# The first head pair of a chunk-selecting attention kernel ordered by hand, with the preparation of the next two pairs among its steps

## The chip, the cores and the metric

The kernel runs on one core of a Trainium2 chip. The metric is the device time in microseconds (us) of one execution. Five engines run their own instruction queues in order: PE (matrix products and transposes), DVE (vector), ACT (scalar functions), POOL (GpSimd) and SP, which here only issues transfers. Weights are transferred by DMAs that POOL issues, queries, keys and values by DMAs that SP issues.

## The reference

Attention over 4 batches, 8 heads, 768 positions, head dimension 64, in which each query sees only its six best key chunks of 32; then a layer in which each token goes to one of eight experts.

```python
k_min, k_max = k_chunks.min(3), k_chunks.max(3)
ub = sum(maximum(q * k_min, q * k_max))          # per query and chunk
ub = where(causal, ub, -1e9)
top_chunks = argsort(ub)[..., -6:]
scores = 0.125 * q @ k.T
scores = where(chunk chosen and causal, scores, -1e9)
attn_out = softmax(scores) @ v
x = attn_out, heads side by side                 # 3072 x 512
e = argmax(x @ w_gate)                           # one expert per token
out = softmax weight * relu(x @ w1[e]) @ w2[e]
```

## The kernel before

**Tiling.** The 32 heads are handled as 16 pairs (NP = 16, four pairs to a batch), numbered by `i`. A pair's keys, queries and values come as 128 x 6 x 2 x 64 tiles, each by two loads of 192 KB (L199 to L203). There is one buffer for keys and one for queries, so the load for the next pair can begin only when PE has transposed the present one; values have two buffers.

**Steps of a pair.** They are the functions of `prep_steps` (L205 on). `k_t(hf)` transposes half of the keys on PE into a PSUM tile (three buffers, tag "m", shared by most steps). `k_red` takes the chunk maximum and minimum on DVE, `k_out` copies the keys into KTE on ACT. `q_t` transposes queries, `q_v` copies them (DVE), `q_r` takes their positive part (POOL), `q_c` and `q_s` write both heads into QSB (POOL, ACT). `kse` prepares the chunk bounds (DVE), `ub` multiplies with them (PE, eight passes, L320) and copies the result (ACT). `select_t`, `select` and `mask` choose six chunks: transposes (PE), `max` (DVE), transposes again, and two copies into the mask rows of QSB (ACT). `mask_rows` writes the matching rows of KTE once per buffer.

Then come seven units per pair: `scores(i, u)` (PE, exponential on ACT, causal masking on POOL for units 0, 1, 5 and 6), `av(i, u)` (product with the values, PE), `add(i, u)` (sum for the denominator, DVE), `out_t` (DVE), and the router steps of the pair before (`ud`, `lgp_t`, `lgp`, `x_t`, `xr`).

**Order.** In the main loop (L779 on) PE and POOL run in the order in which the code is written (`manual_schedule(engines={PE, POOL})`); the other engines' order is found by a scheduler. The loop does, for pair i, its own scores, the selection for pair i + 1 and the key and query preparation for pair i + 2. `keys(j)` is the key part of that, and issues the load of the keys of pair j + 1.

**The prologue** (L740 to L778) comes before the loop, with POOL, DVE and ACT in written order too. `consts_first` starts nine matrix products on zeros (`warm_up`), builds identity, iotas and causal offsets, and clears buffers. `first` transposes pair 0's keys and queries. `consts_pool` makes further constants on POOL, `ub` and `select_first` handle pair 0's selection in two halves, so that scores of the first half (`scored`) run between them. Then pair 1's keys and queries are prepared whole, and `consts_last` ends it. The loop's pass for i = 0 has its own branches: no work of an earlier pair, and `keys(2)` after `out_t`.

**Weights.** `load_w` (L180) moves a quarter of one expert's weights (512 KB as bf16, converted on the way) by a DMA from POOL; 32 of them fill `w_all`. `weights(slot)` (L707) issues those that fall in a slot; the 44 slots lie four to a pair, in pairs 0 to 13 except 5, 9 and 13. All 32 are spread evenly over them. After the last pair the expert stage gathers token rows and multiplies them with the weights.

Of the kernel before, what the change touches and what calls it, by code (L numbers as in the profile page):

```python
# [24 lines left out]
def kernel(  # L25
# [32 lines left out]
    W1W = WE // 2  # L58
    DC = 2 * E
    CW = 64  # L60

    const = ctx.enter_context(tc.tile_pool(name="const", bufs=1))
    dram = ctx.enter_context(tc.tile_pool(name="dram", bufs=1, space=bass.MemoryType.DRAM))
# [54 lines left out]
    def warm_up():  # L118
        wb = work.tile([128, 512], BF16, tag="Pr", bufs=4, name="wb")
        nc.vector.memset(wb[:], 0.0)  # L120
        pw = ps_o.tile([128, 512], FP32, tag="o", name="pw")
        for n in range(9):
            nc.tensor.matmul(pw[:], lhsT=wb[:, 0:128], rhs=wb[:], start=True, stop=True)

    def consts_first():
        warm_up()
        nc.gpsimd.memset(warm[:], 0.0)
        nc.scalar.activation(warm[:], warm[:], AF.Exp)
        masks.make_identity(nc, ident_f[:])
        iota(iota_p[:], [[0, 1]], mul=1)  # L130
        iota(colc[:], [[1, NCH], [0, CH]])
        iota(iota_c[:], [[1, NCH]])
        zero_half(KTE[0])
        nc.gpsimd.memset(KS[0][:], 0.0)
        nc.gpsimd.memset(KD[0][:], 0.0)
        zero_half(QSB[0])
        nc.gpsimd.memset(nsel[:].rearrange("p t h a n -> p (t h a n)").bitcast(FP32), 0.0)
        nc.vector.tensor_scalar(pm64[:], iota_p[:], 64.0, None, ALU.subtract)
        nc.vector.tensor_scalar(chunk_p[:], iota_p[:], 32.0, None, ALU.is_ge)
        nc.vector.tensor_scalar(tmp_p[:], iota_p[:], 64.0, None, ALU.is_ge)  # L140
        nc.vector.tensor_tensor(chunk_p[:], chunk_p[:], tmp_p[:], ALU.add)
        nc.vector.tensor_scalar(tmp_p[:], iota_p[:], 96.0, None, ALU.is_ge)
        nc.vector.tensor_tensor(chunk_p[:], chunk_p[:], tmp_p[:], ALU.add)
        nc.vector.tensor_copy(out=ident_b[:], in_=ident_f[:])
        for t in range(NT):
            thr = const.tile([128, 1], FP32, name=f"thr{t}")
            nc.vector.tensor_scalar(thr[:], chunk_p[:], float(4 * t), None, ALU.add)
            nc.vector.tensor_scalar(cbias[:, t % 3, t // 3, :], iota_c[:], thr[:, 0:1], NEG,
                                    ALU.is_gt, ALU.mult)
        mask_rows(0)  # L150

    def consts_pool():
        zero_half(KTE[1])
        nc.gpsimd.memset(KS[1][:], 0.0)
        nc.gpsimd.memset(KD[1][:], 0.0)
        zero_half(QSB[1])
        zero_half(KTE[2])
        nc.gpsimd.memset(ones_b[:], 1.0)
        nc.gpsimd.memset(dcol[:], 0.0)
        nc.gpsimd.memset(dcol[:, DC:DC + 1], 1.0)  # L160
        nc.gpsimd.memset(wgb[:], 0.0)
        iota(rev8[:], [[-1, E]], base=E)
        iota(ebase[:], [[NTOK, E]])
        iota(jio[:], [[1, NB]])
        for b in range(B):
            nc.gpsimd.iota(tokid[:, b], pattern=[[384, 2], [128, 3]], base=b * S, channel_multiplier=1)

    def consts_last():
        colf = work.tile([128, 128], FP32, tag="Pr", bufs=4, name="colf")
        iota(colf[:], [[1, 128]])  # L170
        wg_v = moe_w_gate.rearrange("(c p) e -> p c e", p=128)
        nc.sync.dma_start(out=wgb[0:64, :, 0:E], in_=wg_v[0:64])
        nc.sync.dma_start(out=wgb[64:128, :, E:2 * E], in_=wg_v[64:128])
        nc.vector.tensor_scalar(U128[:], colf[:], iota_p[:, 0:1], None, ALU.is_gt)
        nc.vector.tensor_copy(out=base_e[:], in_=ebase[:])
        nc.vector.tensor_scalar(tri8[:, 0, :], rev8[:], float(E) - 0.5, None, ALU.is_ge)
        for e in range(1, E):
            nc.vector.tensor_scalar(tri8[:, e, :], rev8[:], float(E - e) - 0.5, None, ALU.is_ge)

    def load_w(s_):  # L180
        e, n = divmod(s_, 4)
# [23 lines left out]
    def prep_steps(i):  # L205
# [35 lines left out]
        def q_c(hf):  # L241
            nc.gpsimd.tensor_copy(out=qsb[0:64, 0, ts(hf, 384)], in_=s[f"qT{hf}"][0:64, :])  # L242

        def q_s(hf):
            nc.scalar.activation(qsb[0:64, 1, ts(hf, 384)], s[f"qp{hf}"][64:128, :], AF.Copy)

        def first():
            for hf in range(2):
                k_t(hf)
            for hf in range(2):  # L250
                pq = ps_s.tile([128, 2, 512], FP32, tag="s", name="pq")
                s[f"qp{hf}"] = pq[:, 0, 0:384]
                for t in range(3):
                    nc.tensor.transpose(pq[:, 0, ts(t, 128)], s["q"][:, 3 * hf + t], ident_f[:])
            k_red(0)
            k_out(1, 0)
            k_red(1)
            k_out(0, 0)
            k_out(0, 1)
            kse()  # L260
            for hf in range(2):
                qT = s[f"qT{hf}"] = work.tile([128, 384], FP32, tag=f"qT{hf}", name="qT")
                qA = s[f"qA{hf}"] = work.tile([128, 384], FP32, tag=f"qA{hf}", name="qA")
                nc.scalar.activation(qA[:], s[f"qp{hf}"], AF.Relu)
                nc.vector.tensor_copy(out=qT[:], in_=s[f"qp{hf}"])
                nc.gpsimd.tensor_copy(out=qsb[0:64, 0, ts(hf, 384)], in_=qT[0:64, :])
            for hf in range(2):
                nc.scalar.activation(qsb[0:64, 1, ts(hf, 384)], s[f"qp{hf}"][64:128], AF.Copy)
            k_out(1, 1)

        def select_first(filler, scored):
            pt = ps_m.tile([128, 3, 2, 2, 32], FP32, tag="m", name="pt")
            for t in range(3):
                nc.tensor.transpose(pt[:, t], s["ubT"][:, ts(t, 128)], ident_f[:])
# [27 lines left out]
            choose(0)  # L302
            bound(1)
            put(0)
            scored()
            choose(1)
            put(1)

# [36 lines left out]
        def mask():  # L345
            pt = ps_m.tile([64, S], BF16, tag="m")
            for hf in range(2):
                for t in range(3):
# [2 lines left out]
            nc.scalar.activation(qsb[64:64 + NCH, 0, :], pt[0:NCH, :], AF.Copy)  # L351
            nc.scalar.activation(qsb[64:64 + NCH, 1, :], pt[32:32 + NCH, :], AF.Copy)

        return dict(k_t=k_t, k_red=k_red, k_out=k_out, q_t=q_t, q_v=q_v, q_r=q_r, q_c=q_c, q_s=q_s, kse=kse, ub=ub,
                    select_t=select_t, select=select, mask=mask, first=first, select_first=select_first)


# [344 lines left out]
    route = [route_steps(b) for b in range(B)]  # L702
    NW = 4 * E
    slots = [4 * i + g for i in range(NP - 2) for g in range(4) if i < HP or i % HP != 1]
    wq = [slots[n * len(slots) // NW] for n in range(NW)]

    def weights(slot):  # L707
        for n in range(NW):
# [31 lines left out]
    with tc.manual_schedule(engines=MAN):  # L740
        load(0, "k")
        load(0, "q")
        load(1, "k")
        load(0, "v")
        load(1, "q")
        load(1, "v")
        with tc.manual_schedule(engines={POOL, DVE, ACT}):
            consts_first()
            prep[0]["first"]()
            consts_pool()  # L750
            prep[0]["ub"]()
            p = prep[1]

            def scored():
                scores(0, 0)
                scores(0, 1)

            prep[0]["select_first"](lambda: p["k_t"](0), scored)
            mask_rows(1)
            p["k_red"](0)  # L760
            p["k_out"](0, 0)
            p["k_out"](0, 1)
            p["k_t"](1)
            load(2, "k")
            p["k_red"](1)
            p["k_out"](1, 0)
            p["k_out"](1, 1)
            p["q_t"](0)
            p["q_t"](1)
            load(2, "q")  # L770
            for hf in range(2):
                p["q_v"](hf)
                p["q_s"](hf)
                p["q_r"](hf)
                p["q_c"](hf)
            p["kse"]()
            mask_rows(2)
            consts_last()  # L778
        for i in range(NP):  # L779
            b, hp = divmod(i, HP)  # L780
            r = rout[i - 1] if i else None
            pn = prep[i + 1] if i + 1 < NP else None
            j = i + 2
            pj = prep[j] if j < NP else None

            if i:
                av(i - 1, 6)
                out_t(i - 1, 1)
                load(i + 1, "v")
                scores(i, 0)  # L790
                scores(i, 1)
                r["ud"]()
                if pn:
                    pn["q_v"](1)
                    pn["q_r"](1)
                weights(4 * i)
                scatters(i, 0)
                keys(j, lambda: scores(i, 2))
            else:
                scores(i, 2)  # L800
                weights(0)

            av(i, 0)
            scores(i, 3)
# [2 lines left out]
            out_t(i, 0)  # L807
            if pn:
                pn["ub"]()
            if pj and i:  # L810
                pj["kse"]()
            if pn and i:
                pn["q_c"](0)
                pn["q_c"](1)
            weights(4 * i + 1)
            scatters(i, 1)
            early(i, 0)

            if i:
                r["lgp_t"]()  # L820
                r["x_t"](0)
            else:
                keys(j)
                pj["kse"]()
            if pn:
                pn["select_t"]()
            if i:
                r["lgp"]()
                r["xr"](0)
            if pn:  # L830
                pn["select"]()

# [9 lines left out]
            if hp == 0 and b > 0:  # L842
                route[b - 1]["logits"]()

            if i:
                r["x_t"](1)
            if pj:
                pj["q_t"](0)
                pj["q_t"](1)
                load(i + 3, "q")  # L850
            if i:
                r["xr"](1)
            add(i, 4)
            early(i, 2)

# [105 lines left out]
```

## Time and profile before

| | us |
|---|---|
| median of three runs (lowest, highest) | 374.36 (372.47, 374.82) |
| profiled execution | 372.51 |
| its span, first to last instruction | 370.8 |
| first weight load issued | 26.58 |
| transposes of the keys of pair 0, 1, 2, 3 begin | 5.06, 13.63, 28.34, 39.56 |
| distance from pair 3 to 4, and on to pair 15 | 13.5 to 15.9 each |

The profile gives for each engine its busy time and for TensorE the share of full clock that was granted (PEclk; 0.5 is half). The span holds two large stages: the pairs up to about 226 us, and the experts.

```profile
PE 331.5 (89%) x2585; PEld 188.2 (51%) x2585; DVE 215.6 (58%) x759; ACT 226.3 (61%) x368; POOL 235.5 (64%) x330
...
q0 software_dynamic: 17536, 29.42, 41.5%
q1 hardware_dynamic: 120608, 29.91, 41.5%
```

The first line has busy us, share of the span and number of instructions of each engine. The others have, of a DMA queue, packets, MB and share of the 16 DMA engines' span: q0 carries what POOL issues (weights, scatters, gathers), q1 what SP issues. A line of the chain of waits has start, length and what ran; a line of waits has total, count and longest.

### The profile page before, as it was taken

To read this page: it belongs to the slowest core of one execution; us is meant where nothing else is said; L and a number is where in the kernel's file an instruction comes from. 1 tells how busy PE (TensorE), PEld (TensorE's weight loads), DVE (VectorE), ACT (ScalarE), POOL (GpSimd) and SP (SyncE) were. 2 spreads that over 40 slices of the span, in tenths; PEclk is the share of its full clock that TensorE was granted. 3 is DMA by queue.
4 is the path that set the end of the run, shared out by engine and by line. 5 is a ranking of instruction groups with operands and counts; after the bars stand their busy time and mean duration, and the time that the engine had idled before them with its cause. 6 is when DMAs were issued, how large, how long until landed. Compare 5 with 4: busy or idle time off the path is not lost.

```text
span 370.8 us, 7987 instructions
## 1 busy us (share of the span) xinstructions
PE 331.5 (89%) x2585; PEld 188.2 (51%) x2585; DVE 215.6 (58%) x759; ACT 226.3 (61%) x368; POOL 235.5 (64%) x330
## 2 busy tenths in 40 slices
PE   6777999999989999989997998987998989999980
PEld 3335566575665566566564655642543444444430
DVE  8389779779879779888795997842530000000000
ACT  4357787787777878767775775660444444544430
POOL 4564786795879886768965584758175766555331
PEclk9759999999999999999999998996999999999996
DMA  9439999999949999947999921124599999899850
GB/s 179 78 87 174 199 220 198 179 186 216 193 104 150 210 194 204 206 112 143 198 215 182 168 61 42 45 58 100 115 207 220 187 265 204 219 177 217 175 133 35
DMA packets 138184, 59.85 MB, mean 161 GB/s; under 512 B 122779, under 2 KB 130973, under 8 KB 138144
## 3 DMA queue, kind: packets, MB, share of 16 engines
q0 software_dynamic: 17536, 29.42, 41.5%
q1 hardware_dynamic: 120608, 29.91, 41.5%
q8 instruction: 23, 0.38, 0.4%
q14 instruction: 17, 0.14, 0.1%
HBM read 56.14 MB, written 10.51 MB: 180 GB/s over the span
## 4 chain that ended last, share of the span: by engine, by line
PE 37%; POOL 19%; DVE 15%; DMA 12%; issue 10%; ACT 3%; SPq 0%; POOLq 0%; DVEq 0%; ACTq 0%
PE ph L668 8%; PE po L399 8%; PE py L684 7%; DMA k<-in_k_dram 6%; PE ps L377 4%; DVE Pa L411 4%; POOL xs_dram L538 3%; POOL qA L239 3%; POOL QSB L242 3%; POOL Pr L386 3%; PE pu L320 3%; POOL w_all L188 2%; PE pu L426 2%; POOL out_dram L691 2%; DVE xrow L471 2%
## 5 line engine op out<-in xcount | busy, mean ns | idle before, releaser
L382 ACT ACTIVATE Pr<-ps 128x768 f32<-128x768 f32 (+2 forms) x112 | 66.7, 628 | 23.6 <-PE ps L377 22.3
L411 DVE TENSOR_TENSOR Pa<-Pa,Pr 128x768 f32<-128x768 f32 (+2 forms) x80 | 67.9, 849 | 5.7 <-PE po L399 3.0
L399 PE MATMUL po<-Pr,v 128*64 128x384 f32 (+2 forms) x448 | 66.5, 415 | 4.6 <-POOL Pr L386 4.1
L377 PE MATMUL ps<-QSB,KTE 128*64 128x384 bf16 (+2 forms) x576 | 55.5, 299 | 0.6 <-ACT QSB L298 0.6
L386 POOL TENSOR_SCALAR_AFFINE_SELECT Pr<-Pr 128x256 f32<-128x256 f32 x80 | 45.5, 595 | 16.3 <-ACT Pr L382 15.4
L684 PE MATMUL py<-w_all,hT 128*128 x224 | 52.7, 379 | 1.2 <-DMA hT<-h__4958 0.9
L239 POOL TENSOR_SCALAR qA<-qT 128x384 f32<-128x384 f32 x30 | 41.0, 1367 | 17.5 <-DVE qT L235 17.5
L399 PEld LDWEIGHTS po<-Pr,v 128*64 128x64 f32 x448 | 35.4, 143 | 22.1 <-POOL Pr L386 8.2
L377 PEld LDWEIGHTS <-KTE 128*64 128x64 bf16 x576 | 31.9, 111 | 26.4 <-issue 22.4
L224 ACT ACTIVATE KTE<-pt 64x384 bf16<-64x384 f32 x64 | 30.9, 483 | 13.3 <-PE pt L212 10.5
L684 PEld LDWEIGHTS <-hT 128*128 128x128 bf16 x224 | 21.9, 98 | 28.2 <-DMA hT<-h__4958 1.3
L220 DVE TENSOR_REDUCE kmx<-pt 128x12 f32<-128x384 f32 x32 | 17.8, 557 | 27.8 <-PE pt L212 23.9
L382 ACT ACTIVATE Pa<-ps 128x768 f32<-128x768 f32 x32 | 26.0, 812 | 10.3 <-PE ps L377 8.9
L668 PE MATMUL ph<-w_all,KTE 128*128 x120 | 29.8, 394 | 1.2 <-ACT y L690 1.2
L538 POOL DMA_INDIRECT xs_dram<-xrow,sli x24 | 26.8, 1116 | 6.4 <-issue 5.8
L399 PE MATMUL po<-Pa,v 128*64 128x384 f32 x128 | 26.7, 497 | 0.0
L668 PE MATMUL ph<-w_all,QSB 128*128 x104 | 24.6, 379 | 1.1 <-ACT y L690 1.1
L188 POOL DMA_DIRECT2D w_all<-in_moe_w_dram x32 | 25.3, 791 | 0.0
L691 POOL DMA_INDIRECT out_dram<-y,ti x14 | 13.9, 990 | 17.4 <-ACT y L690 14.0
L461 POOL TENSOR_TENSOR lg<-lg,lgt 128x48 f32<-128x48 f32 x24 | 7.5, 314 | 20.8 <-DVE lgt L452 19.8
L668 PEld LDWEIGHTS <-KTE 128*128 128x128 bf16 x120 | 11.9, 101 | 16.3 <-issue 3.0
L405 DVE COPY ot<-po 128x384 f32<-128x384 f32 x32 | 17.6, 549 | 3.0 <-PE po L399 3.0
(203 smaller groups left out, 575.6 us busy)
## 6 DMA issues: line engine op xcount, KB each, us to landing
w_all<-in_moe_w_dram POOLq DMA_DIRECT2D x32, 512.0 KB
k<-in_k_dram SPq DMA_DIRECT2D x32, 192.0 KB, 6.4
q<-in_q_dram SPq DMA_DIRECT2D x32, 192.0 KB, 5.3
v<-in_v_dram SPq DMA_DIRECT2D x32, 192.0 KB, 4.2
xs_dram<-xrow,sli POOLq DMA_INDIRECT x24
out_dram<-y,ti POOLq DMA_INDIRECT x14
xg<-xs_dram,grow POOLq DMA_INDIRECT x12
KTE<-xs_dram,grow POOLq DMA_INDIRECT x8
```

Source lines behind the costliest of these rows:

```text
L188: d = nc.gpsimd.dma_start(out=dst, in_=src.rearrange("(c p) f -> p c f", p=128))
L224: nc.scalar.activation(kte[0:64, hd, ts(hf, 384)], s[f"kp{hf}"][64 * hd:64 * hd + 64, :], AF.Copy, bias=0.0, scale=0.125)
L239: nc.gpsimd.tensor_scalar(qA[:], s[f"qT{hf}"][:], 0.0, None, ALU.max)
L377: nc.tensor.matmul(pv[c:c + CW, hd, :], lhsT=kte[:, hd, ds(kb * 128 + c, CW)], rhs=qsb[:, hd, ds(qb * 384 + 384 - w, w)], start=True, stop ...
L382: nc.scalar.activation(P[:, :, ds(c0, w)], pv, AF.Exp)
L386: nc.gpsimd.affine_select(out=pd, in_=pd, pattern=[[0, 2], [1, 128]], compare_op=ALU.is_ge, fill=0.0, base=0, channel_multiplier=-1)
L399: nc.tensor.matmul(s["po"][64 * hd:64 * hd + 64, 384 - w:384], lhsT=vt[:, kb, hd, :], rhs=P[:, hd, ds(c0, w)], start=first, stop=last and ...
L411: nc.vector.tensor_tensor(acc[:, :, 384 - w:384], acc[:, :, 384 - w:384], P[:, :, ds(c0, w)], ALU.add)
L538: d = nc.gpsimd.indirect_dma_start(out=xs_dram[:], out_offset=bass.IndirectOffsetOnAxis(ap=sli[:, u:u + 1], axis=0), in_=bst[b][f"xrow{u % ...
L668: nc.tensor.matmul(ph[:, fh, :], lhsT=xT[:, c, :], rhs=w_all[:, ds(wo + (c * F + fh * 512), 512)], start=(c == 0), stop=(c == NDC - 1), sk ...
L684: nc.tensor.matmul(py[:], lhsT=hT[:, c, :], rhs=w_all[:, ds(wo + (W1W + c * DM), DM)], start=(c == 0), stop=(c == NFC - 1))
L691: d = nc.gpsimd.indirect_dma_start(out=out[:], out_offset=bass.IndirectOffsetOnAxis(ap=fs[j]["ti"], axis=0), in_=y, in_offset=None, bounds ...
```

## The change

The prologue and the loop's pass for pair 0 become one hand-ordered stretch; the loop starts at i = 1 and loses its branches for i = 0. Inside it:

- `warm_up` returns `idle(n)`, which runs n more products on zeros. There are 14: five behind the query transposes, two ahead of the selection, three behind pair 1's first key transposes, and two on either side of the first scores.
- POOL clears the buffers of pairs 1 and 2 ahead of pair 0's query copies. U128, tri8 and base_e are made on POOL instead of DVE. `mask_rows` for pairs 1 and 2 comes before pair 0's selection.
- In `first` the order changes, and the first query copy goes from DVE to ACT. For pair 1, `q_a` (ACT) takes the place of `q_r` (POOL), and `q_d` (POOL, from the SBUF copy) that of `q_s` (ACT).
- Five weight loads (EARLY) are issued inside the stretch: three behind the constants on POOL, two behind the issue of scores(0, 2). The other 27 are spread over the 44 slots. KB is 1.
- Pair 2's keys are prepared in two parts: the first behind `out_t(0, 0)`, the second behind scores(0, 6). The load of pair 3's keys follows the second.

```diff
-    wq = [slots[n * len(slots) // NW] for n in range(NW)]
+    wq = EARLY * [-1] + [slots[n * len(slots) // (NW - EARLY)] for n in range(NW - EARLY)]
...
+            consts_pool()
+            consts_last()
+            for n in range(3):
+                load_w(n)
+            idle(2)
+            def filler():
+                p["k_t"](0)
+                idle(3)
+            prep[0]["select_first"](filler, idle, lambda: scores(0, 0))
+            scores(0, 1)
+            scores(0, 2)
+            p["k_red"](0)
+            p["k_out"](0, 0)
+            p["k_out"](0, 1)
+            for n in range(3, EARLY):
+                load_w(n)
+            av(0, 0)
+            scores(0, 3)
+            av(0, 1)
+            p["k_t"](1)
+            load(1 + KB, "k")
+            add(0, 1)
+            p["q_t"](0)
+            p["q_t"](1)
+            load(2, "q")
+            p["k_red"](1)
+            p["k_out"](1, 0)
+            p["k_out"](1, 1)
+            for hf in range(2):
+                p["q_v"](hf)
+                p["q_a"](hf)
+            p["kse"]()
+            out_t(0, 0)
+            pj["k_t"](0)
+            scores(0, 4)
+            p["ub"]()
+            pj["k_red"](0)
...
+            p["q_c"](0)
+            p["q_c"](1)
+            p["q_d"](0)
+            p["q_d"](1)
+            weights(0)
+            p["select_t"]()
+            p["select"]()
+            av(0, 2)
+            scores(0, 5)
+            av(0, 3)
+            scores(0, 6)
+            add(0, 3)
+            pj["k_t"](1)
+            load(2 + KB, "k")
+            p["mask"]()
+            weights(1)
+            add(0, 4)
+            pj["k_red"](1)
+            pj["k_out"](1, 0)
+            pj["k_out"](1, 1)
+            av(0, 4)
+            av(0, 5)
+            pj["q_t"](0)
+            pj["q_t"](1)
+            load(3, "q")
+            add(0, 5)
...
+            weights(2)
+            weights(3)
-        for i in range(NP):
+        for i in range(1, NP):
```

The new functions:

```python
def q_a(hf):
    qA = s[f"qA{hf}"] = work.tile([128, 384], FP32, tag=f"qA{hf}", name="qA")
    nc.scalar.activation(qA[:], s[f"qp{hf}"][:], AF.Relu)

def q_d(hf):
    nc.gpsimd.tensor_copy(out=qsb[0:64, 1, ts(hf, 384)], in_=s[f"qT{hf}"][64:128, :])
```

## The prediction

> **What bounds the kernel now.** I read the page's slices first, then the chain of waits around the first pair, the DMA queues beneath it, and the waits of TensorE (PE) over the rest. Pairs of heads are numbered 0 to 15; K2 is the key load of pair 2, W0 to W31 the weight loads. The slices last 9.27 us each:
>
> ```profile
> PE   6777999999989999989997998987998989999980
> PEclk9759999999999999999999998996999999999996
> DMA  9439999999949999947999921124599999899850
> ```
>
> PE is full from slice 4 to the end. In slices 1 and 2 it is two thirds busy, its clock sinks, and the DMA engines have time left. So the front is poor, and what is won there before about 40 us can move all that follows. The waits of PE from 40 to 226 us, where the pairs end, say how much else could be won:
>
> ```profile
> PE pt L349 <- DVE xrow L471: 6.8, 9, 2.4
> PE pt L212 <- DMA k<-in_k_dram: 2.4, 1, 2.4
> PE pr L512 <- DVE oh L492: 1.6, 3, 0.5
> ```
>
> Next the chain of waits, start and length:
>
> ```profile
> 9.41 3.21 PE pu L320 x8
> ...
> 26.90 0.22 PE po L399 x4
> 27.12 1.29 PE pu L320 x8
> 28.41 0.82 PE pt L212 x6
> 29.23 0.02 issue
> 29.24 0.37 SPq L201
> 29.61 0.04 issue
> 29.66 9.77 DMA k<-in_k_dram
> 39.43 0.14 issue
> 39.56 0.85 PE pt L212 x6
> ```
>
> The eight bound products (L320) take 3.21 us near half clock and 1.29 us at full. More telling is the load: K3 is issued at 29.24 and lands at 39.43, just before PE wants it. The same load needed 2.7 us (18.95 to 21.65) when the DMAs were idle. The difference is the three weight loads, issued by GpSimd (POOL) from 26.58 on. The DMA queues from 28 to 33 us, then from 33 to 37:
>
> ```profile
> q0 software_dynamic: 411, 0.81, 103.4%
> q1 hardware_dynamic: 2, 0.00, 0.1%
> ```
> ```profile
> q0 software_dynamic: 541, 0.66, 92.9%
> q1 hardware_dynamic: 516, 0.13, 24.7%
> ```
>
> Weights use q0, keys q1. While weights that were issued earlier are in flight, a key load gets nothing at first, then packets in turn that are small (256 B). It ends about when the weights do.
>
> **The change, part by part.** Up to the first scores: pair 0's first qT copy goes to ScalarE (ACT), so the bound products start at about 8.7, when DVE's KD at 8.58 + 0.09 ends, not 9.41. The second copy, on DVE, still ends at 9.27; three quarters of 1.29 behind it give 10.3 instead of 12.62, if 14 added warm-up products hold the clock: 2.3 us. The steps from 12.70 to 17.97 follow unchanged, so the first exponential ends at 15.6. The warm-ups cost 0.22 us each (half of 4.02/9, the first nine at the slow clock) to 0.43; 3 to 6 us in all, lying in PE waits that the change leaves open (DVE and ACT chains). Without that cover the last two would cost 0.9 us.
>
> mask_rows for pairs 1 and 2 (2 x 0.74 us, 0.99 with POOL busy) go ahead of the selection on DVE; DVE is free from 9.27 to about 11.5 there, so 1.5 to 2.0 fits. POOL's five memsets (10.34 to 12.90) go into its idle stretch 4.63 to 9.33: free. The triangle, offsets and U128 leave DVE (1.2 us at 26.9 to 27.8) and cost POOL some 0.7 us. The two gate loads on SP come some 3 us earlier, long before K2: nothing. q_d on POOL and q_a on ACT replace two 1.2 to 1.3 us POOL maxima of pair 1; ACT work is swapped for POOL work, off the path below.
>
> Now ACT sets the pace: 15.6, mask copy 0.49, exponential of scores(0,1) 0.77, of scores(0,2) 0.81, two key copies 0.98, three transposes 0.45, and waits of about 0.2: K1's second half is read at 19.3 and SP issues K2 at 19.35 (18.95 before). By then scores(0,3) and av(0,1) are done, which stood at 26.9 before. This is a real lead of 7 us.
>
> The weights spend it. POOL's last q_c ends at 9.8 (0.5 after the qT copy), the constants take 1.2 (12.90 to 14.11) + 0.7, so W0, W1, W2 are issued at 11.7 to 13.3, 0.8 apart; W3 and W4 follow the masking of scores(0,1) (exponential over at 17.0, three masks) at 17.5 to 19.1, all ahead of K2. W5 follows the q_c and q_d of pair 1 at about 23.4. Flow starts some 2.2 us after issue (26.58 to 28.8) and moves 0.81 MB in 4.2 us, 195 GB/s: 0.524 MB need 2.7 us. W0 to W4 run from 13.9 to 27.4, with W5 to 30.1. PE's order has pair 2's key transposes ahead of scores(0,4), the bounds of pair 1 and all behind them; they wait for K2. Bounds: K2 lands at 22.1 if it loses nothing (19.35 + 2.7), and at 31.9 if it lands after all six weights (six of 0.524 + 0.39 MB at 197 GB/s from 13.9). The nearest row is K3 above, in the same position behind weights, so I take 30.5, between 29.1 (behind W4, plus 1.7 for its own bytes) and 31.9. PE then stands idle from about 20.3, and all that the front won, clock included, is under that wait.
>
> [...]
>
> From K2's landing L to pair 3's key transposes (39.56 before), at full and half clock: transposes 0.45 or 0.70, scores(0,4) 0.33 or 0.78, bounds 1.29 or 3.21; then ubT and its transposes 1.45 (28.41 to 29.86); selection 0.60 + 1.12 + 0.45 = 2.2; on DVE two adds 1.9 and the reduction of pair 2's second key half 1.03, both ahead of ACT's key copies 1.0 that free the PSUM buffer of the last query transposes 0.5, then av(0,6) 0.65: 5.1; scores(1,0), scores(1,1) and the denominators as before, 39.56 - 36.94 - 0.31 = 2.3. That is L + 13.1 at full clock, L + 15.7 at half. After 10 us of idling it starts at half. Two stretches of 3.4 us (PE busy first, PEclk after POOL):
>
> ```profile
> 16.48:19.88 3.40, 2.62 (x19) 1.84 (x17) 1.57 (x11) 2.05 (x4) 1.17 (x3) 0.50 0.01 2
> 23.31:26.71 3.40, 3.40 (x17) 1.70 (x18) 3.19 (x8) 2.39 (x5) 3.40 (x6) 0.50 0.51 116
> ```
>
> The first, 77% busy, left the clock at 0.50; only the second, busy throughout, was followed by 1.00. I take L + 15.2 = 45.7: 6.1 us later than before.
>
> [...]
>
> Later, five weights fewer in pairs 1 to 12 (24 left, not 29): the one DMA stall of PE, 2.4 us at 197.9, may go (0 to 2.4; a new stall of that size is the bound below nothing). Pairs 11 and 12 issue four weights there instead of five, so I take 2.0. POOL issues 5 x 0.79 us less there, but PE hardly waits for POOL: nothing. Sum: +6.1 - 2.0 = +4.1 on the profiled execution's 372.51, 376.6. That execution lies 1.85 below the median of the three runs, 374.36, so I forecast 378.4.
>
> **The rivals.** (1) K2 slips through. If q1 gets its share as soon as K2 is issued, L is 22.1, the sum L + 13.9 = 36.0: 3.5 us earlier than before, with 2.0 later, -5.5: 368.9. For it: at 40.44 a key load issued at the same time as a weight load landed after 3.6 us. Against: that one was first in the queue, K2 is sixth. It decides if L is below about 25.5, for there the two sums cancel. (2) The lead is lost but repaid. L of 29 with an early clock (13.9) is +3.3; POOL relief and fewer stalls give back 3: about 374.7. Against: PE's idle in the pairs is mostly for DVE. (3) The warm-ups fail to hold the clock, so the front isn't quicker. The products stay at 3.21, K2 is issued about 2 us later, but W0 to W2 no earlier or later; L hardly moves, and it is inside the forecast.
>
> **How the numbers follow.** Forecast (K2 lands with the weights, little repaid): 0.55, own range 375.5 to 382.5, from L 28.5 with 13.9 to L 31.9 with 15.7, less 0 to 2.4. Rival 1: 0.25, 366.5 to 371.5. Rival 2: 0.20, 373 to 377. The range runs from rival 1's middle to the forecast's top, 368.5 to 382.5, and leaves out about 0.2. One per cent, 3.7 us, is what a measurement of this kernel can tell from none: slower takes 0.44 of the forecast and 0.02 of rival 2, faster 0.23 of rival 1 and 0.01 of rival 2, the rest, 0.30, is within it.
>
> **What would show it.** Right: K2's load takes over 9 us, PE waits for k at pair 2's first transposes for 8 to 11 us ending near 30, the clock is 0.5 around it, pair 3's transposes come near 45. The lead: scores(0,3) by 18. Wrong: K2 lands by 25, pair 3's transposes come before 39.6, or the pairs from 60 us on run closer together than the 13.5 to 15.9 us of now.

## The result, and the profile after

Four runs of the changed kernel have a median of 384.87 us (384.19 to 386.81), four of the kernel before, taken beside them, 373.68 (372.47 to 374.82): a ratio of 1.031, 95% interval 1.026 to 1.036. The change makes the kernel some 3% slower. The profiled execution took 384.46 us, its span is 382.7. A few runs further down fell in a second, slower state (one in four of early0_noidle and of pre_early0, two in four of unsplit_early0): the ratios leave these out, the medians do not.

The busy slices of the page, TensorE, its granted clock and the DMA engines; a slice is 9.57 us here:

```profile
PE   7823997999899999999999998978987789999990
...
PEclk9985999999999999999999999996999999999997
DMA  9997299999985899945998932134679699997951
```

Up to 19 us TensorE is somewhat busier than before and its clock is full, and then there is a hole: the third slice (19 to 29 us) has 2, the fourth 3, while the DMA engines stand at 9 and 7. The waits of TensorE, first up to 40 us and then from 40 to 235, where the pairs end:

```profile
PE pt L219 <- DMA k<-in_k_dram: 13.7, 1, 13.7
PE pu L343 <- DVE KD L337: 1.7, 1, 1.7
...
PE pt L372 <- DVE xrow L494: 5.6, 9, 1.0
...
PE pt L219 <- DMA k<-in_k_dram: 1.6, 1, 1.6
```

Before, no key load kept TensorE waiting for 13.7 us anywhere. The chain of waits runs through it:

```profile
20.34 0.48 PE pt L219 x3
...
21.16 0.07 SPq L208
...
21.27 13.75 DMA k<-in_k_dram
...
35.16 0.88 PE pt L219 x3
36.03 0.78 PE ps L400 x4
36.81 2.61 PE pu L343 x8
...
49.16 0.86 PE pt L219 x6
...
51.45 0.52 SPq L208
...
52.01 12.60 DMA k<-in_k_dram
```

SP issues the keys of pair 2 as soon as the second half of pair 1's is transposed (20.34 + 0.48). It does so in two loads, one for each head, at 20.85 and 21.27; the second lands 13.75 us later, at 35.02. Then the bound products (L343) take 2.61 us for the 1.29 of full clock. At 52.01 the next load, that of pair 4, starts the same thing on a smaller scale.

A table by stretch, each from the start of one pair's key transposes. The second columns are from another execution of each kernel, on two other chips (368.41 and 379.52 us):

| stretch, us | before | after | differs | before, 2nd | after, 2nd | differs |
|---|---|---|---|---|---|---|
| start to pair 3 | 39.56 | 49.09 | +9.5 | 39.31 | 49.08 | +9.8 |
| pair 3 to 4 | 13.45 | 15.66 | +2.2 | 13.60 | 15.72 | +2.1 |
| pair 4 to 15 | 159.61 | 156.98 | -2.6 | 156.96 | 156.95 | 0.0 |
| pair 15 to the end | 158.18 | 160.97 | +2.8 | 156.83 | 155.95 | -0.9 |
| span | 370.8 | 382.7 | +11.9 | 366.7 | 377.7 | +11.0 |

The first two rows repeat to 0.3 us and are the loss. The last two do not repeat: the 2.4 us stall on keys at 197.9 of the first execution before is absent from the second, and the end of the program, the same in both kernels, took 155.9 to 161.0.

### The profile page after: what moved, and what is told of

The parts are those of the page before. It is cut to its first block, busy times and chain, and to the rows that moved or that the text cites. A ratio compares the mean times of both kernels' runs of the same rounds, so it can differ in the third digit from the quotient of the medians.

```text
span 382.7 us, 8012 instructions
## 1 busy us (share of the span) xinstructions
PE 332.5 (87%) x2599; PEld 186.1 (49%) x2599; DVE 215.4 (56%) x748; ACT 225.9 (59%) x369; POOL 236.7 (62%) x333
## 4 chain that ended last, share of the span: by engine, by line
PE 34%; POOL 20%; issue 16%; DMA 13%; DVE 11%; ACT 3%; SPq 1%; POOLq 1%; DVEq 0%; ACTq 0%
PE po L422 9%; DMA k<-in_k_dram 7%; POOL xs_dram L561 5%; PE ps L400 5%; PE ph L691 4%; PE pu L449 3%; PE py L707 3%; POOL out_dram L714 3%; POOL Pr L409 3%; PE pu L343 3%; DVE Pa L434 3%; POOL QSB L249 2%; PE pt L219 2%; DMA xs_dram<-xrow,sli 2%; DMA KTE<-xs_dram,grow 2%
## 5 line engine op out<-in xcount | busy, mean ns | idle before, releaser
L422 PE MATMUL po<-Pr,v 128*64 128x384 f32 (+2 forms) x448 | 65.2, 406 | 5.1 <-POOL Pr L409 4.5
L409 POOL TENSOR_SCALAR_AFFINE_SELECT Pr<-Pr 128x256 f32<-128x256 f32 x80 | 47.2, 618 | 29.8 <-ACT Pr L405 28.6
L246 POOL TENSOR_SCALAR qA<-qT 128x384 f32<-128x384 f32 x28 | 37.9, 1353 | 12.1 <-DVE qT L242 12.1
L422 PEld LDWEIGHTS po<-Pr,v 128*64 128x64 f32 x448 | 33.6, 139 | 22.5 <-POOL Pr L409 10.4
L400 PEld LDWEIGHTS <-KTE 128*64 128x64 bf16 x576 | 31.1, 110 | 26.2 <-issue 21.8
L561 POOL DMA_INDIRECT xs_dram<-xrow,sli x24 | 27.9, 1162 | 6.4 <-issue 6.1
L219 PE MATMUL pt<-ident_f,k 128*128 128x128 f32 x96 | 15.1, 292 | 15.3 <-DMA k<-in_k_dram 15.3
L714 POOL DMA_INDIRECT out_dram<-y,ti x14 | 14.0, 1002 | 22.1 <-ACT y L713 20.4
L691 PE MATMUL ph<-w_all,QSB 128*128 x104 | 24.6, 379 | 2.6 <-DMA QSB<-spare 1.4
L249 POOL CAST QSB<-qT 64x384 bf16<-64x384 f32 x32 | 18.6, 609 | 4.6 <-DVE qT L280 2.2
```

Of the source, the lines that this page charges most:

```text
L246: nc.gpsimd.tensor_scalar(qA[:], s[f"qT{hf}"][:], 0.0, None, ALU.max)
L400: nc.tensor.matmul(pv[c:c + CW, hd, :], lhsT=kte[:, hd, ds(kb * 128 + c, CW)], rhs=qsb[:, hd, ds(qb * 384 + 384 - w, w)], start=True, stop ...
L409: nc.gpsimd.affine_select(out=pd, in_=pd, pattern=[[0, 2], [1, 128]], compare_op=ALU.is_ge, fill=0.0, base=0, channel_multiplier=-1)
L422: nc.tensor.matmul(s["po"][64 * hd:64 * hd + 64, 384 - w:384], lhsT=vt[:, kb, hd, :], rhs=P[:, hd, ds(c0, w)], start=first, stop=last and ...
L561: d = nc.gpsimd.indirect_dma_start(out=xs_dram[:], out_offset=bass.IndirectOffsetOnAxis(ap=sli[:, u:u + 1], axis=0), in_=bst[b][f"xrow{u % ...
L691: nc.tensor.matmul(ph[:, fh, :], lhsT=xT[:, c, :], rhs=w_all[:, ds(wo + (c * F + fh * 512), 512)], start=(c == 0), stop=(c == NDC - 1), sk ...
```

## The experiments

The theory to test (A): the five early weight loads lie ahead of K2 in the DMA engines and delay it; the rest of the change gives a lead that this wait swallows. The rival (B): the hand-written order itself is the loss, for instance the two-part preparation of pair 2 or the added products. Ratios are to the kernel before, run on the same chip.

**Weights alone, order alone.** The first three kernels part the change. *early0* issues no weight early:

```diff
-    EARLY = 5
+    EARLY = 0
-            for n in range(3):
+            for n in range(min(3, EARLY)):
```

> The changed kernel without the five early weight loads (EARLY = 0; all 32 spread over the slots as before). Theory A, the weights hold K2 back: K2, issued at about 20.8 us, lands after some 2.7 us as it did before the change, PE waits 2 to 3 us instead of 13.7, pair 3's key transposes come near 37 (39.56 before, 49.09 changed), and the time is 368 to 373, the stall of 2.4 us late in the pairs being back. Theory B, the single key buffer and the order that puts pair 2's keys ahead of scores(0,4) cost the time whoever uses the DMAs: PE still waits 8 us or more and the time stays above 379.

*early0_noidle* leaves out the 14 added warm-up products besides:

```diff
-            for _ in range(n):
+            for _ in range(n if n == 9 else 0):
```

> As the run without early weights, and without the 14 added products on zeros too (the nine at the start stay). If they hold the clock: the bound products of pair 0 take about 3.2 us again, the granted clock is 0.5 for most of 9.6 to 26 us, and pair 3's key transposes come 2 to 3 us later than with them. If they do not matter, the two runs agree within 0.5 us up to pair 3.

*before_early5* is the kernel before with nothing of the change but its five early weights, three behind `consts_pool`, two behind `select_first`:

```diff
+            for n in range(3):
+                load_w(n)
...
+            for n in range(3, 5):
+                load_w(n)
...
-    wq = [slots[n * len(slots) // NW] for n in range(NW)]
+    wq = 5 * [-1] + [slots[n * len(slots) // (NW - 5)] for n in range(NW - 5)]
```

> The kernel before with one part of the change alone: three weight loads behind POOL's constants, two behind the first scores, 27 in the slots. Theory A: K2, issued at about 19, lands near 32 to 35 instead of 21.65, pair 2's key transposes (28.34 before) wait for it, and the time is 376 to 382. Theory B: the weights run in DMA time that was idle, and the time is 370 to 374, as before or better by the 2.4 us stall that goes.

A second execution of the kernel before stands beside them:

> The kernel before once more, for its expert stage. In the first execution 115.0 us lay between the first expert product and the end, in the changed kernel's 119.9. If that is chance of one execution, this run differs from 115.0 by some us; if it belongs to the change, it repeats 115.0 within 1.

| kernel | us | ratio [95%] | pair 2, 3, 4 begin | PE waits for K2 |
|---|---|---|---|---|
| changed | 384.87 | 1.031 [1.026, 1.036] | 35.2, 49.1, 64.8 | 13.7 |
| early0 | 371.78 | 1.012 [1.007, 1.016] | 24.6, 40.4, 58.0 | 3.1 |
| early0_noidle | 376.19 | 1.021 [1.013, 1.030] | 27.8, 43.5, 60.8 | 3.1 |
| before_early5 | 377.09 | 1.027 [1.023, 1.031] | 35.1, 46.8, 60.6 | 6.7 |
| before_again | 368.41 | one run | 28.3, 39.3, 52.9 | none |

The early weights, put alone into the old order, cost nearly the whole loss; without them more than half of it goes. Theory A holds for the wait. But early0 was to have pair 3 near 37 and to gain; pair 3 came at 40.4, and the kernel is 1% slower than before: a second loss is in the order. Its chain of waits shows where:

```profile
20.32 0.48 PE pt L219 x3
...
21.14 0.07 SPq L208
...
21.26 3.19 DMA k<-in_k_dram
...
24.58 0.87 PE pt L219 x3
25.45 0.78 PE ps L400 x4
26.23 2.62 PE pu L343 x8
```

K2 now needs 3.19 us for its second load, with the DMA engines to itself (3.6 from the issue of the first, at 20.83, to the end), and since SP can issue it only when pair 1's keys are transposed, TensorE waits even so. After that wait the bound products take 2.62 us, double, and pair 3 comes 15.8 us after pair 2. K4 is waited for too, 3.1 us.

What before_early5 adds: there K2 is issued at 17.87, ahead of the fourth to seventh weight load. The transfers in the order of their issue (when the issuing began, how long the engine was at it, its line, what):

```profile
14.15 2.47 POOL L188 DMA_DIRECT2D w_all<-in_moe_w_dram  x3
...
17.87 1.00 SPq L201 DMA_DIRECT2D k<-in_k_dram  x2
18.17 1.47 POOL L188 DMA_DIRECT2D w_all<-in_moe_w_dram  x2
...
25.59 1.54 POOL L188 DMA_DIRECT2D w_all<-in_moe_w_dram  x2
```

K2 landed at 34.9 all the same. The DMA queues between 23 and 28 us say why:

```profile
q0 software_dynamic: 783, 0.79, 92.2%
q1 hardware_dynamic: 782, 0.20, 29.9%
```

For each weight packet (1 KB here, near 2 KB from 29 us on) there is one packet of q1 (keys and queries, 256 B): 783 and 782, a fifth of the bytes. From 29 to 34 us, when more has moved (2.1 MB) than the three weight loads issued ahead of K2 hold (1.57), it is still 461 and 462: the weights issued after the keys move between them just the same. In the changed kernel the same queues look thus from 20 to 25 us, from 27 to 28 and from 33 to 34:

```profile
q0 software_dynamic: 828, 0.89, 114.0%
...
q1 hardware_dynamic: 7, 0.00, 0.3%
...
q0 software_dynamic: 103, 0.19, 99.0%
q1 hardware_dynamic: 102, 0.03, 19.4%
...
q1 hardware_dynamic: 1063, 0.27, 118.9%
q0 software_dynamic: 10, 0.01, 7.7%
```

Nearly nothing at first (7 packets in the window, the first at 24.57, 3.7 us after K2's issue; in early0, with no weights in flight, the first came after 1.05), then one for one, and ten times the rate once the weights are through. K2 lands, at 35.02, just behind the last weight packet, which ends at 33.92.

**How much each weight costs.** *early3* has `EARLY = 3` and is otherwise the changed kernel. *late_slots* keeps the five but issues the other 27 from pair 2 on, so that none is issued between K2 and pair 2:

```diff
-    slots = [4 * i + g for i in range(NP - 2) for g in range(4) if i < HP or i % HP != 1]
+    slots = [4 * i + g for i in range(2, NP - 2) for g in range(4) if i < HP or i % HP != 1]
```

> The changed kernel with three early weight loads, not five. If K2 lands only when every weight load issued before or soon after it has drained, at about 2.8 us each, K2 lands near 29.5 (35 with five, 24.5 with none) and PE waits 8 us. If the queues took turns by packet from K2's arrival on, it would land about as late as with five, 33 or more.

> The changed kernel with its five early weight loads, and the other 27 from pair 2 on instead of from pair 0 on. Two questions. W5, issued at 24.4 in the changed kernel: if it stands ahead of K2 although K2 was issued at 20.8, K2 lands about 2.7 us earlier without it, near 32. K4, the second wait of 1.7 us: if the weights of pairs 0 and 1 delay it, pair 4's transposes follow pair 3's by 13.4 to 13.8 us instead of 15.7. Both together: about 5 us below the changed kernel, 1.013 of before. If K4 is late only because the value loads ahead of it on SP are, the distance stays above 15.

Early weights, and the start of pair 2's transposes: five and a sixth at 24.36 (changed kernel) 35.2, five (late_slots) 32.3, three and one at 24.3 (early3) 27.1, none and one at 24.3 (early0) 24.6. The sixth load of 512 KB, issued 3.5 us after K2 (20.85), held up K2, two loads of 192 KB, by 2.9 us. The fourth and fifth cost 2.6 each, if the one at 24.3 in early3 cost nothing there; the first three, largely through when K2 is issued, 2.5 together. For early3 this is neither of the two forecasts: K2 landed at 27.0. The ratios were 1.021 [1.017, 1.025] for late_slots and 1.005 [1.002, 1.008] for early3. late_slots was to reach 1.013: K2 came as early as forecast, but half clock lasted 8.8 us behind it, pair 3 came 15.4 us after pair 2, not 13.9, and half of the lead was gone. In late_slots K4 no longer kept TensorE waiting, and pair 3 to pair 4 took 14.03 us, not 15.66: the weights issued at 45.2, 48.2 and 51.3 were what made K4 late in the changed kernel.

**The clock after the wait.** *warm_early0* is early0 with 14 more products (a constant tile by KTE, into a score buffer that nothing reads) ahead of pair 2's first key transposes, so that TensorE is busy while it waits:

```diff
             out_t(0, 0)
+            pz = ps_s.tile([128, 2, 512], FP32, tag="s", name="pz")
+            for _ in range(14):
+                nc.tensor.matmul(pz[:, 0, :], lhsT=ident_b[:], rhs=KTE[0][:, 0, 0:512], start=True, stop=True)
             pj["k_t"](0)
```

> The changed kernel without early weights, with 14 products of no use (into a score buffer) ahead of pair 2's first transposes, where PE waits 3.1 us for K2. Theory: part of the 15.8 us from pair 2's to pair 3's transposes is the half clock that this wait brings (0.50 from 23.9 to 34.1). With the clock held it should be about 12 to 13, as with K2 loaded ahead (12.0), though K2 lands no earlier; pair 3 near 37, the time 2 to 4 us below the run without them. If the wait alone is the cost, it stays at 15 to 16.

Windows of five us, first early0, then warm_early0 (PE busy first; PEclk, the granted clock, third from the end):

```profile
25.00:30.00 5.00, 4.32 (x18) 1.66 (x16) 1.02 (x2) 1.87 (x4) 0.27 (x1) 0.50 0.69 117
30.00:35.00 5.00, 5.00 (x30) 2.44 (x28) 4.01 (x18) 1.65 (x4) 1.20 (x1) 0.59 0.00 0
```

```profile
25.00:30.00 5.00, 4.32 (x32) 2.05 (x33) 2.61 (x16) 2.64 (x5) 0.28 (x1) 1.00 0.72 116
30.00:35.00 5.00, 5.00 (x53) 3.18 (x49) 4.87 (x10) 3.94 (x8) 3.49 (x5) 1.00 0.38 82
```

From 25 to 30 us TensorE does 32 products in place of 18 in the same busy time. Pair 3 came 11.97 us after pair 2, not 15.79: a wait of 3 us for keys was followed by half clock that cost another 3.8. But the time did not fall (372.87, ratio 1.015 [1.010, 1.019]): K4 was then waited for, 3.8 us, and the step from pair 11 to 12 took 17.99 us instead of 14.18, for a cause that stays open.

**The two-part preparation of pair 2.** *unsplit_early0* is early0 with both halves of pair 2's keys behind `out_t(0, 0)`, and the load of K3 there too (the reductions and copies of the second half move with them):

```diff
             pj["k_t"](0)
+            pj["k_t"](1)
+            load(2 + KB, "k")
             scores(0, 4)
...
             add(0, 3)
-            pj["k_t"](1)
-            load(2 + KB, "k")
```

> The changed kernel without early weights, with pair 2's two key halves transposed, reduced and copied together behind out_t(0, 0), and pair 3's key load issued there, as the loop does. If the split is what stretches pair 0 (its DVE reduction behind two adds, its copies behind that, the last query transposes behind those), pair 3's transposes come 2 to 4 us earlier than 40.37 and the time falls by as much against the run without early weights. If the half clock is what stretches it, they come within 1 us of 40.37.

Pairs 2, 3 and 4 at 24.8, 39.3, 53.3, no wait for K4; the four runs took 366.35, 368.15, 373.98 and 374.17 against 368.55 (365.31 to 369.74) of the kernel before: too scattered for a ratio. Pair 3 came 1.1 us earlier than in early0, between the two forecasts. In the profiled execution pair 15 began at 210.1, 5.7 us earlier than in early0 (215.8) and as in before_again (209.9). So the rival B is right about a second cause: the new order spends its lead on the early wait, the clock after it and a late K4. How much of this is the split itself the run doesn't separate: with it the load of K3 was issued at 26.3 and not at 34.9, and half clock lasted 2.9 us behind the wait, not 9.6.

**The warm-up products in the changed kernel.** *after_noidle* leaves out the 14 products there:

> The changed kernel with its five early weights, without the 14 added products on zeros. As the prediction had it: the front is slower by some 2 to 3 us, but K2 is bound by the weights, so it still lands near 35, and the time is the changed kernel's within 1.5 us. If the products matter here too, K2 lands 2 us or more later, or the half clock lasts longer, and the time is 2 to 5 us above.

It took 376.9, ratio 1.026 [1.021, 1.031], and the changed kernel, run once more, 378.49, 1.027 [1.020, 1.034]: no difference that these intervals show, though in the profiled executions pair 15 began 4.0 us earlier without the products (217.7 and 221.7). Between the two kernels with no early weights the same products brought pair 3 forward by 3.1 us. Without them K2 is issued 2 us later, at 22.8, but lands 3.8 earlier, at 31.2, because the sixth weight load moves to 26.3 and its packets come when K2 is through (from 29 to 30 us the queues move 7 weight packets and 1,103 of keys and queries).

> The changed kernel once more, beside the kernel before on this chip and in one set with the next three. Theory: K2 lands near 35 and PE waits 13 to 14 us again, and the time is 1.03 of before. Its expert stage took 119.9 us from the first expert product to the end, against 113.7 to 115.0 in five other executions. If that was chance of one execution, it is 113.5 to 115.5 here and the ratio may sink to 1.02; if it belongs to the change, it is 119 to 121 again.

**The wait taken away.** *pre_early0* loads the keys and queries of pair 2 in the prologue, behind pair 1's, into a part of `w_all` whose weights come last. The loads of pair 3 take the places that those of pair 2 had, behind pair 1's transposes. There are no early weights. *pre_early5* is the same with the five:

```diff
+        if i == 2 and nm in ("k", "q"):
+            t_ = w_all[:, ds((E - 1) * WE + (1536 if nm == "q" else 0), 1536)].bitcast(FP32).rearrange(
+                "p (t h d) -> p t h d", t=NT, h=2)
+        else:
...
             load(1, "v")
+            load(2, "k")
+            load(2, "q")
...
-            load(1 + KB, "k")
+            load(2 + KB, "k")
...
-            load(2, "q")
+            load(3, "q")
```

> The changed kernel without early weights, and with K2 and pair 2's queries loaded right behind pair 1's, into the part of the weight buffer that is filled last; so later key and query loads are issued one buffer earlier too. Theory C, the wait for K2 and the half clock that it leaves behind are what eats the lead of the front: PE never waits for K2, the granted clock stays at 1.0 from 20 to 35 us, pair 3's key transposes come near 35 (40.37 with the wait, 39.3 before), and the time is 0.98 to 0.99 of before, or 1.00 if K4 lands late behind the weights of pair 0. Theory D, the woven order itself is longer: pair 3's transposes stay 15 us behind pair 2's, and the time stays above before.

> As the run before, with the five early weight loads back. Theory A: with no transfer of pair 2 behind them they cost nothing at pair 2; K3, issued near 21, lands with the weights near 33 to 36, just when it is wanted (0 to 2 us of wait), and the time is within 2 us of the run without them. If the early weights harm in another way, the time is over 1.02 of before as in the changed kernel.

| kernel | us | ratio [95%] | pair 2, 3, 4 begin |
|---|---|---|---|
| pre_early0 | 363.32 | 0.987 [0.979, 0.996] | 23.0, 35.0, 50.1 |
| pre_early5 | 364.00 | 0.989 [0.986, 0.992] | 23.0, 35.2, 50.2 |

With K2 there in time the order of the change is about 1% faster than before, and the five early weights do no harm any more: in pre_early5 K3 stands where K2 stood, issued at 20.8, its first load landing at 33.0, and TensorE doesn't wait for it at pair 3 (35.2). What TensorE waits for in pre_early0, up to 60 us:

```profile
PE pt L223 <- ACT KTE L235: 1.5, 1, 1.5
PE pu L347 <- DVE KD L341: 1.5, 1, 1.5
...
PE pt L223 <- DMA k<-in_k_dram: 1.0, 1, 1.0
```

The wait for K2 is gone; 1.5 us for ACT's copies of pair 1's keys and 1.0 for K4 are left. Two kernels are to take away the latter: *pre_unsplit* (pre_early0 with the edit of unsplit_early0) and *pre_early5_late* (pre_early5 with that of late_slots).

> Both repairs in one, without early weights: K2 and pair 2's queries loaded ahead, and pair 2's key halves prepared together. K4's wait of 1.0 us and the 15.1 us from pair 3's to pair 4's transposes should go to about 13.6, pair 4 near 48.5 (50.1 without the second repair, 52.9 before), and the time to 0.98 of before. If the second repair only moves the wait, it is 0.987 as without it.

> K2 and pair 2's queries loaded ahead, five early weights, the other 27 from pair 2 on. If the weights of pairs 0 and 1 are what delays K4, its wait of 1.1 us goes, pair 4's transposes come near 48.7 (50.2 with those weights, 52.9 before), and the time is 0.982 to 0.986 of before; if not, 0.989 as with them.

Both lost the K4 wait and gained nothing: 364.14, 0.988 [0.984, 0.993], and 363.59, 0.989 [0.985, 0.993]. In pre_unsplit a wait for DVE's selection, 1.5 us, came ahead of pair 3 instead; in pre_early5_late pair 4 began 1.5 us earlier, at 48.7, and pair 15 at 207.0 as before.

**Why the front's lead was short.** The bound products began at 10.08 and not at 8.7, waiting for KD on DVE. DVE's steps in front of that, in the changed kernel (start, length, line, operation):

```profile
4.72 0.73 DVE L155 TENSOR_SCALAR cbias<-iota_c,thr 128x24 f32<-128x24 f32 x1
...
5.49 0.67 DVE L155 TENSOR_SCALAR cbias<-iota_c,thr 128x24 f32<-128x24 f32 x1
6.18 1.24 DVE L117 TENSOR_SCALAR KTE<-colc,pm 24x768 bf16<-24x768 bf16 x2
```

and what POOL does meanwhile:

```profile
4.68 1.44 POOL L113 MEMSET KTE<- 64x768 f32 x2
6.08 0.76 POOL L113 MEMSET QSB<- 64x768 f32 x1
```

In the kernel before, the last two threshold steps (L148 there) took 0.24 each, the mask rows (L115) 0.74 the pair. Next to POOL's memsets, moved to 4.68, the first of the two steps lasts as long as one memset (0.72), the others 0.4 to 0.5 longer than before. The profile before had shown the same thing already: there, too, earlier threshold steps take 0.57 and 0.71 beside a memset, and 0.24 with none.

```profile
2.49 0.73 POOL L111 MEMSET KTE<- 64x768 f32 x1
2.69 0.57 DVE L148 TENSOR_SCALAR cbias<-iota_c,thr 128x24 f32<-128x24 f32 x1
...
3.58 0.73 POOL L111 MEMSET QSB<- 64x768 f32 x1
3.63 0.71 DVE L148 TENSOR_SCALAR cbias<-iota_c,thr 128x24 f32<-128x24 f32 x1
...
4.72 0.24 DVE L148 TENSOR_SCALAR cbias<-iota_c,thr 128x24 f32<-128x24 f32 x1
...
5.30 0.74 DVE L115 TENSOR_SCALAR KTE<-colc,pm 24x768 bf16<-24x768 bf16 x2
```

*held_memsets* is the changed kernel with the memsets held until DVE has written pair 0's mask rows, by a copy that reads them; *pre_held* has the same edit in pre_early0:

```diff
         mask_rows(0)
+        nc.gpsimd.tensor_copy(out=KS[1][64:64 + NCH, 0:1], in_=KTE[0][64:64 + NCH, 1, 0:1])
         zero_half(KTE[1])
```

> The changed kernel, with POOL's five memsets for pairs 1 and 2 held until DVE has written the mask rows of pair 0 (a copy of one column of those rows stands ahead of them on POOL); nothing is left out. Theory (the memsets, moved to 4.68, stop DVE's small writes from buffer to buffer beside them: 0.73 and 0.67 for what took 0.24, 1.24 for 0.74): DVE's last threshold step takes 0.24 again, KD is ready at 8.7 and not 10.0, the bound products start at 8.7 to 8.8, the memsets lie at 6.1 to 8.6, W0 is issued at about 12.0 (13.27), K2 at 19.4 to 19.6 (20.84), K2 lands at 33.5 to 34 (35.0) because the weights start 1.3 earlier, and the time is 1 to 1.5 us below the changed kernel's, a ratio near 1.023. Rival (DVE was late by its own order or by the warm-up products, not by POOL): KD stays at 9.8 to 10.0, W0 comes later than 13.27, and the time is the changed kernel's or up to 1 us above.

> The kernel with the keys and queries of pair 2 loaded in the prologue and no early weights, with the same held memsets. Theory: bound products at 8.7, pair 2's transposes at 21.6 to 22 (23.0), pair 3's at 33.6 to 34 (35.0), and the time 1 to 1.5 us less than that kernel's ratio of 0.987, near 0.984. Rival (the gain of the front is taken up by another wait, of pair 2's transposes for ACT's key copies or by K3's): pair 2 at 22.5 or later or pair 3 within 0.4 of 35.0, ratio as before, 0.987.

DVE's same steps in held_memsets:

```profile
4.71 0.24 DVE L155 TENSOR_SCALAR cbias<-iota_c,thr 128x24 f32<-128x24 f32 x1
...
5.04 0.24 DVE L155 TENSOR_SCALAR cbias<-iota_c,thr 128x24 f32<-128x24 f32 x1
5.29 0.74 DVE L117 TENSOR_SCALAR KTE<-colc,pm 24x768 bf16<-24x768 bf16 x2
```

They are back at 0.24 and 0.74. The bound products began at 8.87, W0 was issued at 11.99, K2 at 19.6, and pair 2 began at 33.06, 2.1 us earlier than in the changed kernel, somewhat more than expected. Pair 15 was 2.2 us earlier too (219.5); the ratio, 1.024 [1.020, 1.029], can't be told from the changed kernel's. In pre_held pairs 2 and 3 began at 21.7 and 33.7, 1.3 us earlier than in pre_early0 (0.8 of it was left at pair 15), and its ratio is the lowest of all: 360.65 us (359.63 to 363.21) against 367.28, 0.984 [0.978, 0.989]. That interval overlaps those of the other kernels with K2 loaded ahead, so the start times show the gain over them, and the ratio doesn't. Its slices:

```profile
PE   7879999999998999989998999968999899999980
...
PEclk9999999999999999999999999998999999999996
```

No hole, and full clock through the whole front.

## Why the prediction was right in kind and too small in size

The prediction said slower, by K2 landing behind the weights; that mechanism is shown by before_early5, early0 and pre_early5. The time, 384.87, lies above its range, 368.5 to 382.5. In the profiled executions +4.1 us were predicted and +11.95 came. Step by step:

- **What bounds the kernel.** Right: what the front gains lasts. In pre_held pair 4 began 5.1 us earlier than in before_again (47.8, 52.9) and pair 15 4.2 (205.7, 209.9), 1.1% of the time; the rest of its 1.6% would be the end of the program, which varies by itself.
- **"POOL's five memsets go into its idle stretch: free."** Wrong, and the first failure. POOL was idle there, but DVE was not: the memsets made DVE's writes 1.4 us longer, so KD, the second query copy, W0 (13.27 for 11.7) and K2's issue (20.85 for 19.35) all came 1.3 to 1.6 us late. Held back, they give 2.1 us of K2's landing. A threshold step took 0.73 for 0.24 beside memsets of 0.72 each; by what way the one holds up the other, no run shows.
- **K2's landing, 30.5 taken between 29.1 and 31.9.** The second failure: the upper bound was the rule. It had six weights and K2, 3.54 MB, move at 197 GB/s from 2.2 us behind W0's issue. The pace was right: from 13.27 + 2.2 to the landing at 35.02 the DMA engines moved 3.89 MB, 199 GB/s. W0 was 1.6 us later than in the sum, 1.3 of it for the memsets (11.99 when they are held). And 0.35 MB more than in the sum went through, 1.8 us at that pace, nearly all of it queries of pair 2, issued at 21.97 right behind K2 on the same queue, which the sum doesn't have; whether K2 would land earlier without them no run shows. Of the 4.5 us the choice below the bound is 1.4, the late W0 1.6, these bytes 1.8, less 0.3 for pace and rounding. The lower end, "behind W4", fails by late_slots: even without the sixth weight K2 landed at 32.15, 30.6 with W0 where the sum had it, and not 29.1. The other bound, 22.1, was too early by 0.9: 2.7 us is the time of one of K2's two loads, and both together need 3.6 (early0).
- **Nothing at first, then packets in turn.** Right: 7 packets of keys in five us (20 to 25), then 102 beside 103 of the weights in one us. The zero that the prediction saw is a late start: K2's first packet moves 3.7 us after its issue (20.85, 24.57), and so does K3's in the kernel before (29.24, 32.94); in late_slots, after_noidle, held_memsets and before_early5, too, none of K2's packets moves in the first 3.1 us. With no weights in flight it is 1.05 (early0; in the kernel before 18.95, 20.01). In two more, where the weights ran out sooner, it was 2.4 and 2.9 (early3, unsplit_early0). Why, no run here settles.
- **From K2's landing to pair 3, 15.2.** 14.1 came (35.02 to 49.09). Half clock lasted 4.9 us behind the wait here, 9.6 in early0, where it cost 3.8; the bounds 13.1 to 15.7 held, the choice between them was too slow by 1.1.
- **Pair 3 to 4: no cost seen.** The third failure: +2.2. The step "24 left, not 29" counted the later weights by number and not where they fall against K4. In the changed kernel K4 (51.44) is issued behind three of them (45.24, 48.19, 51.31); in the kernel before it was issued (40.44) ahead of those near it (40.74, 42.43, 45.21).
- **"I take 2.0" off for the stall at 197.9.** Wrong in kind: the second execution of the kernel before has no such stall, and from pair 4 to 15 the two then agree to 0.01 us. One trace had shown a chance event, and it was booked as a gain.
- **The lead.** scores(0, 3) at 19.2 and not by 18, for the memsets; the warm-ups hold the clock as assumed (1.00 from 5.9 to 26.4 us; 3.1 us at pair 3 without early weights), and it is true that all of it lay under the wait for K2.
- **The range.** The forecast's own lower end, 375.5, doesn't follow from its terms: L 28.5 with 13.9, less 2.4, gives 374.8. Its upper end, 382.5, took no term for the memsets and none for pair 3 to 4, and the measured time lies 2.4 above it.
- **The rivals.** K2 slipping through (1) is refuted by the queues. Repayment later (2) too: between the second executions the only later stretch that is shorter is the end, by 0.9, and the end alone varies by 5. Warm-ups without effect (3): they held the clock, but they also moved W5 ahead of K2's end, so that K2 landed 3.8 us later with them; the time shows neither.

## What to carry to other kernels

A transfer that nobody waits for is not free because its own deadline is far: price it by the small load on the chain that will be in flight with it, whether it is issued before or after (a wait of 13.7 us for K2 here, 2.9 of it by the one weight load issued behind it). Before an order is packed tighter, bring the loads that it will want sooner forward as well: the same order with the same early weights lost 3% with K2 late and won 1.1% with K2 in time. And an engine's idle stretch is free only for work that doesn't slow a neighbour: look at the lengths of the instructions beside it (here 0.73 us for 0.24), not at the gap alone.

## What the runs showed of the hardware unasked

- Keys and queries alone move 1,062 to 1,103 packets of 256 B in a us (held_memsets, changed kernel, late_slots, after_noidle), beside weights 86 to 169, one for each weight packet (changed kernel, after_noidle, before_early5).
- After TensorE had waited for keys the half clock lasted 2.9, 3.9, 4.9, 8.8 and 9.6 us (unsplit_early0, early3, changed, late_slots, early0), with much the same work behind the wait. The whole stretch at 0.5 in the records was 3.4, 6.8, 13.7, 17.1 and 10.2 us, multiples of 3.4, as are those of the kernel before (9.65 to 13.06, 16.48 to 26.72, 224.69 to 228.10). In pieces of 3.41 us, TensorE was busy in these three for 87%, for 77, 44 and 100%, and for 100%, and in the changed kernel (26.37 to 40.02) for 0, 0, 43 and 81%: full clock came behind the pieces with 81, 87, 100 and 100%, and behind none of those with 0, 0, 43, 44 and 77%. In early0 the pieces from 23.9 on were 80, 80 and 100% busy, with 0.7 us of idling in the second, behind the wait, and full clock came behind the third; in before_early5 it did not come behind two of 82 and 83%. What decides between them, no run shows.
- The end of the program, the same instructions in every kernel, took 155.9 to 161.0 us from pair 15 on in the two executions each of the kernel before and the changed one, and 153.4 to 157.4 in the others; a difference of 1% between two single profiles can be this alone.
